# Sigmoid attention and a gated feed-forward layer on one core: score tiles in bursts of three, the last sigmoid put off, and row copies in mid-stretch

## The chip, the core and the metric

The kernel runs on one core of one Trainium2 chip. The time is device microseconds, the median of several runs. TensorE (PE) multiplies matrices, with its weight loads on a row of their own (PEld); VectorE (DVE) and ScalarE (ACT) do elementwise work and empty PSUM, the eight-bank memory that TensorE writes to; GpSimd (POOL) and SyncE (SP) here issue DMA transfers. Each engine works through its instructions in the order in which the program gives them and waits on semaphores for the others.

## What is computed

Eight batches of twelve heads, 448 positions, head size 64. Attention uses a sigmoid in place of a softmax; its output, 3584 tokens of width 768, goes through a feed-forward layer of width 2048 with a SiLU gate.

```python
scores = scale * np.matmul(q, k.transpose(0, 1, 3, 2)) - np.log(S)
attn = 1.0 / (1.0 + np.exp(-scores))
attn_out = np.matmul(attn, v)                     # (8, 12, 448, 64)
x = attn_out.transpose(0, 2, 1, 3).reshape(B * S, H * D)
h = x @ w_in                                      # (3584, 768) @ (768, 2048)
g = h * (1.0 / (1.0 + np.exp(-h)))
out = g @ w_out                                   # (3584, 2048) @ (2048, 768)
```

## The kernel before

**Attention.** Four heads at a time make a block `g`, three blocks to a batch, 24 in all; a block has seven key chunks `ch`, so there are 168 score tiles (`units`). `scores(g, ch)` (L170) issues eight matmuls of 64x64 by 448 columns, two quads of four; the four of a quad use four quarters of the TensorE array at once. A tile fills one two-bank PSUM buffer of the pool `ps_sc` (two such buffers), and one sigmoid of 128x896 on ScalarE (L184) reads it into `attnT` (12 buffers). `values(g)` (L194) multiplies the seven tiles of a block with v in 28 matmuls (L208) into two single banks, and VectorE copies them, scaled, into `xT` (L219). Matmuls of 64x64 are called scores and values here, all others dense.

**Feed-forward.** `h_unit(b, fc)` (L230) takes six dense matmuls of 448 columns (L236) into one single bank, a sigmoid on ScalarE (`tsig`, L248) and a product on VectorE (`gTr`, L249). `out_set` (L289) computes two 128-row blocks of the output in seven products instead of eight, after Strassen's scheme: VectorE forms sums `S` of blocks of `gTr` (L319, L320, L323, L328), each product is eight dense matmuls of 384 columns (L307), the first product is copied by ScalarE (`m1`, L322), and VectorE adds up the others (`plus`, L315). Sums of the weights (`T`, L278) are formed once. In two of the sets ScalarE also copies a block for later (`kept`, L375).

**PSUM.** `ps_sc` holds two buffers of two banks, `ps_1` four single banks, which take in turn the results of `h_unit`, `out_set`, `values` and of the transposes. A new tile takes the bank that, in the order of the program, was given back first.

**The order.** It is written out by hand. `all_moe` (L380) is a generator that emits the dense work of all batches one matmul (one "step") at a time and yields 189 for a step of `h_unit` and 163 for one of `out_set`. `stretch(ns)` (L399) raises `due` by ns and draws steps until `done` has reached it; `hold` keeps it drawing over the seam from the last h unit to the first product. The main loop (L534) takes two score tiles, a "burst", then at most one block of values and one row copy, and then a stretch whose length depends on the batch that the scores belong to (`paces`, L532). A long stretch of 99 steps stands ahead of the third batch (L538). Behind the last scores the rest of the dense work follows.

**The operands of the scores.** k and q are loaded by DMA from GpSimd's queue (`load`, L71; four buffers each). From block 9 on, VectorE rewrites them to rows (`dma_transpose`, L159, the copy is L163) and a DMA from SyncE's queue transposes them (L164). `after_values` (L440) puts the row copies of block g + 3 on the list `later`; `rows_if_any` (L467) takes one from it at each burst, and behind the q copy loads block g + 4.

Of the kernel before, what the change touches and what calls it, by code (L numbers as in the profile page):

```python
# [11 lines left out]
F32 = mybir.dt.float32  # L12
# [5 lines left out]
def kernel(  # L18
# [9 lines left out]
    nc = tc.nc  # L28
# [42 lines left out]
    def load(names, g, c0=0, c1=NCH):  # L71
        b, iq = divmod(g, NQ)
        for name in names:
            if (name, g) not in flat:
                new_flat(name, g)
            for half in range(2):
                h0 = half * (H // 2) + 2 * iq
                nc.gpsimd.dma_start(  # L78
                    flat[name, g][half * HP : (half + 1) * HP, :, c0:c1].rearrange(
                        "p i c d -> p i (c d)"  # L80
                    ),
                    source[name][b, h0 : h0 + 2].rearrange("i (p c) d -> p i (c d)", c=NCH)[
                        :, :, c0 * D : c1 * D
                    ],
                )
# [73 lines left out]
    def dma_transpose(g, name, copy):  # L159
        if ("k", g) not in qkT:  # L160
            new_qkT(g)
        rows = p3.tile([P, NCH, 2, D], F16, tag=f"{name}r", name=f"{name}r")
        copy(rows, flat[name, g].rearrange("p j c d -> p c j d"))  # L163
        nc.sync.dma_start_transpose(  # L164
            out=qkT[name, g], in_=rows.rearrange("p c j d -> p (c j d)")
        )

    attnT = {}

    def scores(g, ch):  # L170
        attnT[g, ch] = p12.tile([P, 2, S], F16, tag="attnT", name="attnT")
        psc = ps_sc.tile([P, 2, 512], F32, tag="pssc", name="psc")
        for half in range(2):
            own = slice(half * HP, (half + 1) * HP)
            for j in range(2):
                rows = slice(j * D, (j + 1) * D)
                nc.tensor.matmul(  # L177
                    psc[own, j, :S],
                    qkT["k", g][rows, ch, own],
                    qkT["q", g][rows, :, own],  # L180
                    start=True,
                    stop=True,
                )
        nc.scalar.activation(  # L184
            attnT[g, ch], psc[:, :, :S], AF.Sigmoid, bias=bias_s, scale=QKSCALE
        )

    xT = {}
    ready = set()
# [36 lines left out]
    pairs = [half * NQ + iq for iq in range(NQ - 1) for half in range(2)] + [NQ - 1, 2 * NQ - 1]  # L226

    hold = False

    def h_unit(b, fc):  # L230
        nonlocal hold
        hold = b > 0 and fc == NFC - 1
        ph = ps_1.tile([P, 512], F32, tag="ps1", name="ph")
        for at, cc in enumerate(pairs):
            assert b in ready or at < 4
            nc.tensor.matmul(  # L236
                ph[:, :S],
                w_in_sb[:, cc, fc * P : (fc + 1) * P],
                xT[b][:, cc, :],
                start=(at == 0),  # L240
                stop=(at == NCC - 1),
            )
            if at < NCC - 1:
                yield 189
        if fc == NFC - 1:
            h_done.add(b)
        tsig = p3.tile([P, S], F16, tag="tsig", name="tsig")
        nc.scalar.activation(tsig, ph[:, :S], AF.Sigmoid, bias=0.0, scale=ISX)  # L248
        nc.vector.tensor_mul(  # L249
            gTr[:, fc, (b % 2) * S : (b % 2) * S + S], ph[:, :S], tsig  # L250
        )
        yield 189

    rows_of = out.rearrange("(b p c) e -> b c p e", b=B, c=NCH)

# [31 lines left out]
        return [rows_of[2 * m + u // NCH, u % NCH] for u in (2 * g, 2 * g + 1)]  # L287

    def out_set(a1, rows1, a2, rows2, last=False):  # L289
        nonlocal hold  # L290
        lo, hi = slice(0, NHC), slice(NHC, NFC)
        osb = [p4.tile([P, DMODEL], F32, tag="osb", name="osb") for _ in range(2)]
        c11, c12 = (osb[0][:, nh * NO2 : (nh + 1) * NO2] for nh in range(2))
        c21, c22 = (osb[1][:, nh * NO2 : (nh + 1) * NO2] for nh in range(2))
        m1 = p2.tile([P, NO2], F32, tag="m1", name="m1")
        sg = [cpool.tile([P, NHC, P], F16, tag=f"S{i}", name=f"S{i}") for i in range(1, 5)]

        def store(rows, o, cols, engines):
            for at, (row, eng) in enumerate(zip(rows, engines)):
                eng.dma_start(row[:, cols], o[at * HP : (at + 1) * HP, cols])  # L300

        left, right, whole = slice(0, NO2), slice(NO2, DMODEL), slice(0, DMODEL)

        def product(a, w):
            po = ps_1.tile([P, 512], F32, tag="ps1", name="po")
            for fc in range(NHC):
                nc.tensor.matmul(  # L307
                    po[:, :NO2], a[:, fc, :], w[:, fc, :], start=(fc == 0), stop=(fc == NHC - 1)
                )
                if fc < NHC - 1:  # L310
                    yield 163
            return po[:, :NO2]

        def plus(o, po, x, sign=ISX):
            nc.vector.scalar_tensor_tensor(  # L315
                out=o, in0=po, scalar=sign, in1=x, op0=ALU.mult, op1=ALU.add
            )

        nc.vector.tensor_sub(sg[2], a1[:, lo], a2[:, lo])  # L319
        nc.vector.tensor_add(sg[0], a2[:, lo], a2[:, hi])  # L320
        po = yield from product(a1[:, lo], wq[0][0])
        nc.scalar.activation(m1, po, AF.Copy, scale=ISX)  # L322
        nc.vector.tensor_sub(sg[1], sg[0], a1[:, lo])  # L323
        hold = False
        yield 163
        po = yield from product(a1[:, hi], wq[1][0])
        plus(c11, po, m1)
        nc.vector.tensor_sub(sg[3], a1[:, hi], sg[1])  # L328
        if last:
            store(rows1, osb[0], left, (nc.sync, nc.sync))  # L330
        yield 163
        po = yield from product(sg[2], tw[3])
        plus(c22, po, m1)
        yield 163
        po = yield from product(sg[1], tw[2])
        plus(c22, po, c22)
        plus(c12, po, m1)
        yield 163
        po = yield from product(a2[:, hi], tw[4])
        plus(c21, po, c22, -ISX)  # L340
        yield 163
        po = yield from product(sg[0], tw[1])
        plus(c22, po, c22)
        plus(c12, po, c12)
        store(rows2, osb[1], whole, (nc.sync, nc.sync))
        yield 163
        po = yield from product(sg[3], wq[1][1])
        plus(c12, po, c12)
        if last:
            store(rows1, osb[0], right, (nc.sync, nc.scalar))  # L350
        else:
            store(rows1, osb[0], whole, (nc.sync, nc.sync))
        yield 163
# [26 lines left out]
    def all_moe():  # L380
        for m in range(B // 2):
            yield from moe_h(2 * m)
            if m > 0:
                yield from moe_set(m, 0)
            yield from moe_h(2 * m + 1)
            if m == 0:
                yield from moe_set(m, 0)
            yield from moe_set(m, 2)
            yield from moe_set(m, 4)
            if m % 2 == 1:  # L390
                g = NCH - 1
                yield from out_set(
                    kept, row_blocks(m - 1, g), block(g), row_blocks(m, g), m == B // 2 - 1
                )

    stream = all_moe()
    done = due = 0.0

    def stretch(ns):  # L399
        nonlocal done, due  # L400
        due += ns
        while done < due or hold:
            step_ns = next(stream, None)
            if step_ns is None:
                break
            done += step_ns

    first_k = load_first_k()
    new_flat("k", 0)
# [30 lines left out]
    def after_values(g):  # L440
# [20 lines left out]
            load("kq", 9)  # L461
        if g >= 6 and g + 3 < NQB:
            later.extend(((g + 3, "k"), (g + 3, "q")))

    later = []

    def rows_if_any():  # L467
        if later:
            g, name = later.pop(0)
            dma_transpose(g, name, nc.vector.tensor_copy)  # L470
            if name == "q" and g + 4 < NQB and g + 4 > 12:
                load("kq", g + 4)

    def values_if_any():
        if waiting:
# [53 lines left out]
        for do, *what in behind.get(n, ()):  # L529
            do(*what)  # L530

    paces = {1: 1600, 2: 2000, 3: 2550, 4: 3400, 5: 3400, 6: 3000, 7: 3000}  # L532
    stretch(paces[1])
    for n in range(NT_B + 3, len(units), 2):  # L534
        burst = units[n : n + 2]
        if n == 2 * NT_B:
            values_if_any()
            stretch(21500)  # L538
        for u in burst:
            scores(*u)  # L540
        values_if_any()
        rows_if_any()
        for g, ch in burst:
            if ch == NCH - 1:
                waiting.append(g)
        if n in (24, 30):
            transposes(4 + (n - 24) // 6, "k")
        elif n in (26, 32):
            transposes(4 + (n - 26) // 6, "q")
        stretch(paces[1] if 1 not in ready else paces[n // NT_B])  # L550
    for g in waiting:
        values(g)
    for _ in stream:
# [31 lines left out]
```

## Time and profile before

| | |
|---|---|
| median of 3 runs | 382.56 us (382.36 to 382.85) |
| the profiled execution | 382.75 us, of which the span of the instructions is 381.0 |
| h steps, L236 | 768 matmuls of 128x448 |
| output steps, L307 | 784 matmuls of 128x384 |
| score and value matmuls, L177 and L208 | 672 and 672, 64x64 by 448 |
| score sigmoid, L184 | 168 of 128x896, mean 1016 ns, 158.9 us |
| tsig, L248, and its product, L249 | 128 each, mean 545 and 623 ns |
| sums of products, L315 | 112, mean 555 and 552 ns |
| xT, L219 | 48, mean 619 ns |
| row copies, L163 | 30 on VectorE, mean 610 ns |
| k loads, q loads | median 5.5 and 5.8 us from issue to landing |

The kernel has an opening of some 77 us, in which the weights are loaded, the first batches' scores run almost alone and the long stretch of 99 h steps ends. From there to about 325 us bursts and dense stretches take turns. The rest, to 377 us, is dense work alone. A row of the profile shows start, duration, engine, line, operation and count; consecutive instructions of one kind are merged. Durations of matmuls overlap since they are pipelined, so the time that a matmul takes up is read from one start to the next.

### The profile page before, as it was taken

Reading aid. Unit: us, or ns where it says so; the run is one execution under the profiler, and the core shown is the slowest. Engines: PE = TensorE matmul, PEld = TensorE weight load, DVE = VectorE, ACT = ScalarE, POOL = GpSimd, SP = SyncE. Lnnn points to the kernel's source line nnn. Section 1 sums busy time; section 2 is a strip of 40 time slices with the busy share of each in tenths; the row PEclk is TensorE's granted clock in tenths of the full one; section 3 lists DMA queues with packets and bytes.
Section 4 is the critical chain, followed back from the end, with each engine's and each line's share of the span. In section 5 each row is a group of like instructions: output and inputs, shape, how many; then the busy total and the mean of one; then the engine's idle time right before and its main releaser. Section 6 shows DMA issues by size and latency. Waiting matters only on the chain.

```text
span 381.0 us, 7663 instructions
## 1 busy us (share of the span) xinstructions
PE 372.2 (98%) x3083; PEld 186.9 (49%) x3083; DVE 233.8 (61%) x415; ACT 240.0 (63%) x328; POOL 92.9 (24%) x158
## 2 busy tenths in 40 slices
PE   7999999999999999999999999999999999999995
PEld 2444445545554445444555444544455444555663
DVE  2446646996565666556767547735857446656773
ACT  4998886758777875778444686577774787044000
POOL 8855326202752323121311303101100000000000
PEclk9999999999999999999999999999999999999999
DMA  7999999974999936937939859535346300110233
GB/s 112 180 188 204 205 203 181 155 103 101 166 236 232 141 51 97 184 47 75 152 68 191 96 112 122 56 101 74 48 77 105 83 3 2 41 41 2 75 92 83
DMA packets 66403, 42.71 MB, mean 112 GB/s; under 512 B 37056, under 2 KB 62912, under 8 KB 66368
## 3 DMA queue, kind: packets, MB, share of 16 engines
q0 software_dynamic: 28032, 22.69, 42.7%
q1 hardware_dynamic: 38112, 19.31, 28.2%
q8 instruction: 24, 0.39, 0.4%
q10 hardware_dynamic: 224, 0.23, 0.2%
q14 instruction: 11, 0.09, 0.1%
HBM read 45.61 MB, written 11.01 MB: 149 GB/s over the span
## 4 chain that ended last, share of the span: by engine, by line
PE 80%; DMA 12%; DVE 2%; ACT 2%; POOL 1%; issue 1%; DVEq 0%
PE po L307 34%; PE ph L236 29%; PE psc L177 9%; PE pav L208 6%; DMA w_in_sb<-in_moe_w_in_dram 6%; DMA w_out_sb<-in_moe_w_out_dram 5%; DVE gTr L249 1%; DMA ks<-in_k_dram 1%; ACT attnT L184 1%; DMA vf<-in_v_dram 1%; DVE T L278 1%; POOL qf L78 1%; PE pw L135 1%; POOL kf L78 0%; ACT qr L138 0%
## 5 line engine op out<-in xcount | busy, mean ns | idle before, releaser
L184 ACT ACTIVATE attnT<-psc,bias_s 128x896 f16<-128x896 f32 x168 | 158.9, 1016 | 53.3 <-PE psc L177 53.2
L236 PE MATMUL ph<-xT,w_in_sb 128*128 128x448 f16 x768 | 153.2, 353 | 0.0
L249 DVE TENSOR_TENSOR gTr<-ph,tsig 128x448 f16<-128x448 f32 x128 | 78.1, 623 | 72.0 <-ACT tsig L248 71.4
L236 PEld LDWEIGHTS <-w_in_sb 128*128 128x128 f16 x768 | 71.9, 98 | 75.7 <-issue 12.9
L248 ACT ACTIVATE tsig<-ph 128x448 f16<-128x448 f32 x128 | 68.2, 545 | 47.8 <-PE ph L236 46.2
L78 POOL DMA_DIRECT2D vf<-in_v_dram x48 | 28.7, 613 | 140.7 <-PE pav L208 140.2
L307 PEld LDWEIGHTS <-S 128*128 128x128 f16 x448 | 42.3, 98 | 33.9 <-issue 6.8
L315 DVE SCALAR_TENSOR_TENSOR osb<-po,osb 128x384 f32<-128x384 f32 x70 | 37.7, 555 | 25.1 <-PE po L307 24.5
L177 PE MATMUL psc<-qT,kT 64*64 64x448 f16 x672 | 50.4, 362 | 2.5 <-ACT attnT L184 1.2
L219 DVE TENSOR_SCALAR xT<-pav 128x448 f16<-128x448 f32 x48 | 27.7, 619 | 30.3 <-PE pav L208 30.3
L307 PE MATMUL po<-T,S 128*128 128x384 f16 x224 | 40.6, 327 | 0.1
L307 PEld LDWEIGHTS <-gTr 128*128 128x128 f16 x304 | 28.7, 98 | 23.4 <-issue 5.2
L307 PE MATMUL po<-w_out_sb,S 128*128 128x384 f16 x224 | 39.9, 326 | 0.0
L208 PE MATMUL pav<-attnT,vf 64*64 64x448 f16 x672 | 37.9, 349 | 0.4 <-DVE gTr L249 0.4
L78 POOL DMA_DIRECT2D qf<-in_q_dram x48 | 28.9, 612 | 38.1 <-DVE qr L163 16.9
L307 PE MATMUL po<-w_out_sb,gTr 128*128 128x384 f16 x192 | 34.7, 327 | 0.0
L177 PEld LDWEIGHTS <-kT 64*64 64x64 f16 x672 | 15.0, 104 | 32.8 <-issue 30.9
L78 POOL DMA_DIRECT2D kf<-in_k_dram x48 | 28.9, 612 | 7.0 <-DVE kr L163 4.4
L208 PEld LDWEIGHTS <-vf 64*64 64x64 f16 x672 | 20.2, 107 | 12.4 <-issue 1.9
L315 DVE SCALAR_TENSOR_TENSOR osb<-po,m 128x384 f32<-128x384 f32 x42 | 23.2, 552 | 4.1 <-PE po L307 2.5
L322 ACT ACTIVATE m<-po 128x384 f32<-128x384 f32 x14 | 6.9, 491 | 23.7 <-PE po L307 23.7
L307 PE MATMUL po<-T,gTr 128*128 128x384 f16 x112 | 21.4, 326 | 0.0
(40 smaller groups left out, 131.0 us busy)
## 6 DMA issues: line engine op xcount, KB each, us to landing
out_dram<-osb SPq DMA_DIRECT2D x54, 192.0 KB, 2.9
qf<-in_q_dram POOLq DMA_DIRECT2D x48, 112.0 KB, 5.8
vf<-in_v_dram POOLq DMA_DIRECT2D x48, 112.0 KB, 4.8
kf<-in_k_dram POOLq DMA_DIRECT2D x46, 112.0 KB, 5.5
w_in_sb<-in_moe_w_in_dram POOLq DMA_DIRECT2D x4, 768.0 KB, 10.5
w_out_sb<-in_moe_w_out_dram POOLq DMA_DIRECT2D x4, 768.0 KB, 17.0
kT<-kr SPq DMA_TRANSPOSE x18, 5.6
qT<-qr SPq DMA_TRANSPOSE x18, 6.2
```

The costliest lines, as they stand in the source:

```text
L78: nc.gpsimd.dma_start(flat[name, g][half * HP : (half + 1) * HP, :, c0:c1].rearrange("p i c d -> p i (c d)"), source[name][b, h0 : h0 + 2] ...
L135: nc.tensor.matmul(pw, dummy[:, :P], dummy, start=True, stop=True)
L177: nc.tensor.matmul(psc[own, j, :S], qkT["k", g][rows, ch, own], qkT["q", g][rows, :, own], start=True, stop=True,)
L184: nc.scalar.activation(attnT[g, ch], psc[:, :, :S], AF.Sigmoid, bias=bias_s, scale=QKSCALE)
L208: nc.tensor.matmul(pav[half][j * D : (j + 1) * D, :S], flat["v", g][own, j, ch, :], at[own, j, :], start=(ch == 0), stop=(ch == NCH - 1),)
L219: nc.vector.tensor_scalar_mul(xT[b][:, half * NQ + iq, :], pav[half][:, :S], SX)
L236: nc.tensor.matmul(ph[:, :S], w_in_sb[:, cc, fc * P : (fc + 1) * P], xT[b][:, cc, :], start=(at == 0), stop=(at == NCC - 1),)
L248: nc.scalar.activation(tsig, ph[:, :S], AF.Sigmoid, bias=0.0, scale=ISX)
L249: nc.vector.tensor_mul(gTr[:, fc, (b % 2) * S : (b % 2) * S + S], ph[:, :S], tsig)
L307: nc.tensor.matmul(po[:, :NO2], a[:, fc, :], w[:, fc, :], start=(fc == 0), stop=(fc == NHC - 1))
L315: nc.vector.scalar_tensor_tensor(out=o, in0=po, scalar=sign, in1=x, op0=ALU.mult, op1=ALU.add)
L322: nc.scalar.activation(m1, po, AF.Copy, scale=ISX)
```

## The change

A burst has three score tiles in the batches that `TILES` names, and two in the second and fourth batch and wherever a block of values is due in the burst. In a burst of three the first tile goes into two single banks of `ps_1`, read by two sigmoids of 128x448; the other two use `ps_sc`. The sigmoid of the third is put off: it is issued behind the next tsig or m1, or when the stretch has drawn more than 1300 ns of steps, or at the stretch's end. In `stretch` an h step now counts 0.72 of its 189 ns (from the third batch on) and an output step 1.28 of its 163, so there are fewer steps between bursts among output steps and more among h steps. `hold` sets in one h unit earlier from the third batch on. The long stretch keeps its length. Besides the row copy at the burst, another is taken from `later` in the middle of each stretch. The output's arithmetic is the same.

```diff
-    def scores(g, ch):
+    late = []
+
+    def late_sigmoid():
+        while late:
+            to, psc = late.pop()
+            nc.scalar.activation(to, psc, AF.Sigmoid, bias=bias_s, scale=QKSCALE)
+
+    def scores(g, ch, banks=None, put_off=False):
         attnT[g, ch] = p12.tile([P, 2, S], F16, tag="attnT", name="attnT")
-        psc = ps_sc.tile([P, 2, 512], F32, tag="pssc", name="psc")
+        if banks is None:
+            psc = ps_sc.tile([P, 2, 512], F32, tag="pssc", name="psc")
+            banks = [psc[:, j] for j in range(2)]
+            parts = [(attnT[g, ch], psc[:, :, :S])]
+        else:
+            parts = [(attnT[g, ch][:, j], banks[j][:, :S]) for j in range(2)]
...
-        nc.scalar.activation(
-            attnT[g, ch], psc[:, :, :S], AF.Sigmoid, bias=bias_s, scale=QKSCALE
-        )
+        if put_off:
+            late.extend(parts)
+            return
+        for to, psc in parts:
+            nc.scalar.activation(to, psc, AF.Sigmoid, bias=bias_s, scale=QKSCALE)
+
+    def single_banks():
+        return [ps_1.tile([P, 512], F32, tag="ps1", name="psc1") for _ in range(2)]
...
     def h_unit(b, fc):
-        nonlocal hold
-        hold = b > 0 and fc == NFC - 1
+        nonlocal hold, weight
+        weight = H_WEIGHT if b > 1 else 1.0
+        hold = b > 1 and fc >= NFC - 2 or b == 1 and fc == NFC - 1
...
         nc.scalar.activation(tsig, ph[:, :S], AF.Sigmoid, bias=0.0, scale=ISX)
+        late_sigmoid()
...
+    H_WEIGHT, SET_WEIGHT = 0.72, 1.28
...
     def out_set(a1, rows1, a2, rows2, last=False):
-        nonlocal hold
+        nonlocal hold, weight
+        weight = SET_WEIGHT
...
         nc.scalar.activation(m1, po, AF.Copy, scale=ISX)
+        late_sigmoid()
...
     def stretch(ns):
         nonlocal done, due
         due += ns
+        middle = due - ns / 2
+        since = 0
         while done < due or hold:
             step_ns = next(stream, None)
             if step_ns is None:
                 break
-            done += step_ns
+            done += step_ns * weight
+            since += step_ns
+            if since > 1300:
+                late_sigmoid()
+            if done > middle:
+                rows_if_any()
+                middle = math.inf
+        late_sigmoid()
...
-    paces = {1: 1600, 2: 2000, 3: 2550, 4: 3400, 5: 3400, 6: 3000, 7: 3000}
-    stretch(paces[1])
-    for n in range(NT_B + 3, len(units), 2):
-        burst = units[n : n + 2]
-        if n == 2 * NT_B:
-            values_if_any()
-            stretch(21500)
-        for u in burst:
-            scores(*u)
+    TILES = {2: 3, 3: 2, 4: 3, 5: 3, 6: 3, 7: 3}
+    paces = {1: 1600, 2: 2400, 3: 2550, 4: 3500, 5: 3300, 6: 3100, 7: 2900}
+    def burst(n, tiles):
+        new = units[n : n + (tiles if not waiting else 2)]
+        for i, u in enumerate(new):
+            single = i == len(new) - 3
+            scores(*u, single_banks() if single else None, len(new) == 3 and i == 2)
         values_if_any()
         rows_if_any()
-        for g, ch in burst:
-            if ch == NCH - 1:
-                waiting.append(g)
+        waiting.extend(g for g, ch in new if ch == NCH - 1)
+        return len(new)
...
+    values_if_any()
+    stretch(21500)
+    n = 2 * NT_B
+    while n < len(units):
+        ns = paces[n // NT_B]
+        tiles = burst(n, TILES[n // NT_B])
+        n += tiles
+        stretch(ns * tiles / 2)
```

More of the change, by code (lines that the diff above doesn't have):

```diff
@@ L177, in scores @@
                 nc.tensor.matmul(
-                    psc[own, j, :S],
+                    banks[j][own, :S],
                     qkT["k", g][rows, ch, own],
@@ L228 @@
     hold = False
+    weight = 1.0
     def h_unit(b, fc):
-        nonlocal hold
-        hold = b > 0 and fc == NFC - 1
+        nonlocal hold, weight
+        weight = H_WEIGHT if b > 1 else 1.0
+        hold = b > 1 and fc >= NFC - 2 or b == 1 and fc == NFC - 1
         ph = ps_1.tile([P, 512], F32, tag="ps1", name="ph")
@@ L394, in all_moe, with rows_if_any @@
                 )
+    later = []
+    def rows_if_any():
+        if later:
+            g, name = later.pop(0)
+            dma_transpose(g, name, nc.vector.tensor_copy)
+            if name == "q" and g + 4 < NQB and g + 4 > 12:
+                load("kq", g + 4)
     stream = all_moe()
@@ L463, in after_values @@
             later.extend(((g + 3, "k"), (g + 3, "q")))
[L465 to L472, printed above, removed]
     def values_if_any():
@@ L530 @@
             do(*what)
-    paces = {1: 1600, 2: 2000, 3: 2550, 4: 3400, 5: 3400, 6: 3000, 7: 3000}
-    stretch(paces[1])
-    for n in range(NT_B + 3, len(units), 2):
-        burst = units[n : n + 2]
-        if n == 2 * NT_B:
-            values_if_any()
-            stretch(21500)
-        for u in burst:
-            scores(*u)
+    TILES = {2: 3, 3: 2, 4: 3, 5: 3, 6: 3, 7: 3}
[5 more added lines that the diff above has]
+            scores(*u, single_banks() if single else None, len(new) == 3 and i == 2)
         values_if_any()
         rows_if_any()
-        for g, ch in burst:
-            if ch == NCH - 1:
-                waiting.append(g)
+        waiting.extend(g for g, ch in new if ch == NCH - 1)
+        return len(new)
+    stretch(paces[1])
+    for n in range(NT_B + 3, 2 * NT_B, 2):
+        burst(n, 2)
         if n in (24, 30):
@@ L549 @@
             transposes(4 + (n - 26) // 6, "q")
-        stretch(paces[1] if 1 not in ready else paces[n // NT_B])
+        stretch(paces[1])
+    values_if_any()
[6 more added lines that the diff above has]
+        stretch(ns * tiles / 2)
     for g in waiting:
```

## The prediction

> **What bounds the kernel now.** First the page's busy shares, then who TensorE waited for, then its timeline in the dense part, then ScalarE and VectorE beside it.
>
> ```profile
> span 381.0 us, 7663 instructions
> PE 372.2 (98%) x3083; PEld 186.9 (49%) x3083; DVE 233.8 (61%) x415; ACT 240.0 (63%) x328; POOL 92.9 (24%) x158
> ...
> PEclk9999999999999999999999999999999999999999
> ```
> ```profile
> PE psc L177 <- ACT attnT L184: 1.2, 4, 0.5
> ...
> PE pav L208 <- DVE gTr L249: 0.4, 1, 0.4
> ```
> TensorE is busy for 98% at a full granted clock, and its waits for other engines sum to a few us, most of them in the first 80. Pipelined busy time says nothing of lost steps, so I read starts:
>
> ```profile
> 204.87 0.57 PE L177 MATMUL psc<-qT,kT 64*64 64x448 f16 x8
> 205.37 1.96 PE L307 MATMUL po<-T,S 128*128 128x384 f16 x11
> ...
> 208.89 0.57 PE L177 MATMUL psc<-qT,kT 64*64 64x448 f16 x8
> 209.29 1.49 PE L208 MATMUL pav<-attnT,vf 64*64 64x448 f16 x28
> 210.72 2.45 PE L307 MATMUL po<-w_out_sb,S 128*128 128x384 f16 x14
> ...
> 214.74 3.58 PE L236 MATMUL ph<-xT,w_in_sb 128*128 128x448 f16 x18
> 218.25 0.57 PE L177 MATMUL psc<-qT,kT 64*64 64x448 f16 x8
> ```
> ```profile
> 331.14 18.32 PE L236 MATMUL ph<-xT,w_in_sb 128*128 128x448 f16 x96
> 349.30 2.76 PE L307 MATMUL po<-w_out_sb,gTr 128*128 128x384 f16 x16
> 351.90 2.76 PE L307 MATMUL po<-T,S 128*128 128x384 f16 x16
> ```
> Undisturbed, an h step takes (349.30 - 331.14)/96 = 0.189 us and an output step 2.60/16 = 0.163. The 18 h steps from 214.74 take 3.51 to the next score matmul, 18 x 0.189 = 3.41 and 0.10 over; the start records give 0.283 from an h step to a score step, so 0.094 over, and 0.256 from an output step, 0.093 over. That is the way into the 64x64 shape. A burst of two tiles lasts 0.503 to the next dense step (204.87 to 205.37), of which the first quad of four concurrent matmuls takes 0.212 by the records and the last, with the way out, 0.291. With the 28 value matmuls it is 1.83 (208.89 to 210.72). Apart from these switches every dense step after 80 us is at its floor, with two exceptions, one of which is this:
>
> ```profile
> 143.78 0.38 PE L177 MATMUL psc<-qT,kT 64*64 64x448 f16 x4
> 144.64 0.38 PE L177 MATMUL psc<-qT,kT 64*64 64x448 f16 x4 [0.48 <-ACT attnT L184]
> 144.95 0.50 PE L307 MATMUL po<-w_out_sb,gTr 128*128 128x384 f16 x2
> ```
> Two bursts stand six output steps apart, the second score buffer is still being read, and the burst lasts 1.17 for 0.50: 0.67 lost. The other is 0.23 at 79.7, where the third product waits for its VectorE difference (L319). So TensorE is the limit, and only switches and these 0.90 can be won.
>
> **The switches saved.** Everything up to the first 99 h steps stays in the same order (77 us of the span), and so does what follows the last scores. In between, TensorE's instruction order of the built kernels, counted, has 63 bursts of two before and 50 after, 26 of three and 24 of two. Groups of 64x64 work: before 46 score bursts x 0.503 + 17 with values x 1.827 + one of values alone 1.42 = 55.6 us, and 64 ways in x 0.094 = 6.0. After: 26 x (0.503 + 0.212) = 18.6, 6 x 0.503 = 3.0, 16 x 1.827 = 29.2, one score-value-score group 1.827 + 0.424 = 2.25, 1.42, sum 54.5; 50 ways in, 4.7. Difference **2.42 us**. The third quad has no row of its own; the bounds are 0.188 (a value quad, (1.42 - 0.10)/7) and 0.291 (a last quad), and I take 0.212, the same pair of operations one quad earlier.
>
> **The other edits by themselves.** 26 tiles are read by two 128x448 sigmoids in place of one 128x896: at best 2 x 0.44 (start to start after a tsig, 214.34 to 214.78) against 0.895 between four in a row (below), at worst 2 x 0.545 against 1.016, 0.07 more each, at most 1.9 us of ScalarE's 140 idle ones. The weights, paces and `hold` issue nothing; they move bursts. The 30 row copies on VectorE (0.61), their 30 DMA transposes on SP and the loads they release on POOL are the same in number; the second of each pair moves to the middle of a stretch, past VectorE's next product sums, SP's output stores and POOL's loads. With 61% of VectorE busy this is free unless a bank waits behind it, which is priced next.
>
> **New waits on the path.** ScalarE's and VectorE's timelines give durations in a queue:
>
> ```profile
> 142.69 3.70 ACT L184 ACTIVATE attnT<-psc,bias_s 128x896 f16<-128x896 f32 x4
> ```
> ```profile
> 210.82 1.16 DVE L219 TENSOR_SCALAR xT<-pav 128x448 f16<-128x448 f32 x2 [1.59 <-PE pav L208]
> 211.90 0.61 DVE L163 COPY kr<-kf 128x896 f16<-128x896 f16 x1
> 212.42 1.67 DVE L315 SCALAR_TENSOR_TENSOR osb<-po,osb 128x384 f32<-128x384 f32 x3
> ```
> Four sigmoids in 3.70: 0.895 from one to the next, 1.016 for the last. xT 0.54 each, a row copy 0.52, then a product sum of 0.555. A sigmoid starts 0.49 after its burst's first matmul (208.89 to 209.39). A long burst's late sigmoid therefore ends at 0.49 + 2 x 0.45 + 0.895 + 1.016 = 3.30 after the burst began. The tightest spacing is 17 output steps: the next burst begins at 0.715 + 17 x 0.163 + 0.094 = 3.58, its second quad at 3.79, its third at 4.00. That is clear, with these exceptions, found by laying each burst's waits against those sums:
> - Twice a `kept` copy (L375, 0.56 in a queue) stands before the late sigmoid and the next burst is a short one: ready at 3.86 + 0.04, wanted at 3.79: 0.11 x 2 = 0.22. Queued behind it are only that burst's values, which are late by the same.
> - In the one score-value-score group, m1 of the product that just ended goes first (ends 0.50 after), two sigmoids end at 0.50 + 0.895 + 1.016 = 2.41 + 0.04, and the second tile wants its buffer at 0.42 + 1.32 + 0.21 = 1.95: 0.50.
> - Once a long burst follows values after 12 output steps (12 x 0.163 + 0.094 = 2.05), and its second single bank is freed by a sum that stands behind two xT and the k copy: 0.10 + 2 x 0.54 + 0.52 + 0.555 + 0.04 = 2.30: 0.25. The q copy now comes behind this sum, not before it.
> - At h steps a single bank is freed 1.40 after its h unit ended (tsig 0.20 later, 0.545, product 0.62, in the records); the closest burst comes 1.47 after: 0 to 0.05, taken as 0.05.
> These sum to 1.02. Gone are the 0.67 at 143.78, since those bursts move apart, and the 0.23 at 79.7, since the first burst now comes after 14 output steps and the difference is finished within it.
>
> **Sum**, against the profiled execution's 382.75: 382.75 - 2.42 + 1.02 - 0.90 = 380.45. The median of the runs, 382.56, is 0.19 lower than that execution: 380.26, so **380.3 us**. If none of the new waits arose it would be 379.2; with all at the rival's prices 381.9.
>
> **The rivals.**
> *ScalarE sets the pace of the long bursts.* Three tiles need three times 0.9 there while TensorE needs 0.715. With the mean durations of the page (1.016, 0.545, 0.634, 0.555) in place of queued ones: the two `kept` places lose 0.50 each, the score-value-score group 0.71, a pair of long bursts 14 steps apart 0.24, the single-bank places 0.49 and 0.23, in sum 2.67 and a gain of 0.65: 381.9. For it: in the 17-step stretches ScalarE would be busy 2.8 to 3.4 of 3.58. Against: four in a row took 3.70, not 4.06. The Trainium skill (TensorEngine Tiling (Array Packing), PSUM Bottleneck) speaks for it: packing small matmuls speeds TensorE and not the emptying of PSUM, which may become the limit. By that rule the time is this 381.9; the trace bears it out at 143.78 alone.
> *The general banks run short.* Two of four are lent to a tile, and 12 of the 26 long bursts take one whose source ended under 2.2 us before. If evacuation took there what the slowest tenth takes now by the records (2.0 for an h unit, 1.75 for a product), 1.3 would go: 381.6.
> *The change does not save the switch.* If the third quad costs 0.291 like a last one, 26 x 0.08 = 2.1 goes: 382.4, no change.
> *Slower: a row copy that waits for its load blocks VectorE.* Loads are otherwise four blocks ahead, but those of block 10 are issued on POOL right behind the values of block 6, and its k copy is now due 8.8 us after those (10.4 before, 102.58 against 92.2), ahead of the sum that frees the single bank of the 12-step place. The second half of k was issued at 94.39 and landed after 6.24, which is 8.4 after the values; the copy is due 0.4 later. Each us later is a us on TensorE: from a landing of about 8.9 us on, the kernel is slower than before. k loads issued from 104 to 112 took up to 8.6, a q transpose 10.5; at 10.5 it is 3.9 more: 384.2. Against it: the loads ahead of it on POOL do not change.
>
> **How the numbers follow.** Forecast 0.62, own range 379.6 to 381.2; ScalarE 0.13; banks 0.08; no switch saved 0.07; slower 0.08; 0.02 for better still. Within 0.2% (0.8 us, about what a measurement of this kernel can tell) lie the third rival and half of the first, 0.07 + 0.065, and of the forecast's share I count 0.06 there and 0.02 as slower, for a wait that the sums above overlook: same 0.20, slower 0.10, faster 0.70. The range reaches from no new waits, 379.2, to just past the third rival, 382.5.
>
> **What would show it.** Right: 50 bursts after the first 99 h steps, long ones of 0.71 us with 0.094 before them, h and output steps at 0.189 and 0.163, and waits of score matmuls for ScalarE of about 0.7 in all behind 77 us. Wrong: long bursts above 0.8 as a rule, h or output steps that wait at their first matmul, a row copy that VectorE waits 1 us or more for near 101, or a late sigmoid that ends after the next burst's third quad.

## The result, and the profile after

The changed kernel takes 379.84 us, the median of six runs (379.45 to 380.55); the kernel before, on the same chip, takes 382.46 (six runs, 382.21 to 382.85). The ratio is 0.9932, with a 95% interval of 0.9919 to 0.9945: faster by 2.6 us. The profiled execution took 379.95 us. The page of the changed kernel, its span, busy shares and granted clock:

```profile
span 378.2 us, 7694 instructions
...
PE 369.5 (98%) x3083; PEld 189.9 (50%) x3083; DVE 234.0 (62%) x415; ACT 243.0 (64%) x354; POOL 93.3 (25%) x158
...
PEclk9999999999999999999999999999999999999999
```

The span is shorter by 2.8 us, the clock is as full as before, and TensorE still has its 3083 matmul instructions and 98%. ScalarE has 26 instructions more, one for each tile that two sigmoids read. Whom TensorE waited for, in us, times and longest:

```profile
PE psc L191 <- ACT attnT L202: 1.1, 4, 0.4
...
PE pav L227 <- DVE gTr L271: 0.4, 1, 0.4
```

By this list next to nothing has changed, so the gain is not in waits that went. It is in what the list does not count, and that is read from starts, in the timeline of TensorE (start, duration, engine, line, operation, tiles, shape, count):

```profile
198.04 0.76 PE L191 MATMUL psc<-qT,kT 64*64 64x448 f16 x12
198.74 1.31 PE L333 MATMUL po<-w_out_sb,S 128*128 128x384 f16 x7
...
202.74 0.76 PE L191 MATMUL psc<-qT,kT 64*64 64x448 f16 x12
203.43 2.61 PE L333 MATMUL po<-T,S 128*128 128x384 f16 x15
...
207.28 0.57 PE L191 MATMUL psc<-qT,kT 64*64 64x448 f16 x8
207.68 1.49 PE L227 MATMUL pav<-attnT,vf 64*64 64x448 f16 x28
209.10 2.77 PE L333 MATMUL po<-w_out_sb,S 128*128 128x384 f16 x16
```

A score tile is one quad: `scores` issues four matmuls (672 for 168 tiles), not the eight in two quads that "The kernel before" gives. A block of values is seven quads. A burst of three lasts from 198.04 to 198.74 and from 202.74 to 203.43: 0.694 by the unrounded records, the median and the least of 26. The burst of two still lasts 0.505. So the third tile costs 0.694 - 0.505 = 0.189, and what remains of a burst when its quads are taken off is 0.505 - 2 x 0.189 = 0.127. Two score tiles with the 28 value matmuls fit the same line: nine quads are 9 x 0.189 + 0.127 = 1.83, and 207.28 to 209.10 is 1.82. The way in is 0.098, read over a whole dense stretch as what it takes to the next score matmul beyond 0.189 and 0.163 a step: 0.094 of it at the last step, the rest mostly at the first, which takes 0.01 longer. Together, a stay in the 64x64 shape costs **0.225 us, however long it is, and 0.189 for each quad**. The price goes with the shape and not with a change of operands: inside a stay the step from scores to values takes 0.189, and the last h step before an output step takes 0.189 too. There were 64 stays, now there are 50.

What else changed are the waits that a group of 64x64 work or a dense stretch shows beyond these floors. From the end of the first 99 h steps to the last scores they sum to 1.11 us before and 1.45 after. Four of them are larger than 0.1 us. The one group in which scores, values and scores follow each other, on TensorE:

```profile
139.78 0.57 PE L191 MATMUL psc<-qT,kT 64*64 64x448 f16 x8
140.18 1.49 PE L227 MATMUL pav<-attnT,vf 64*64 64x448 f16 x28
141.51 0.36 PE L191 MATMUL psc<-qT,kT 64*64 64x448 f16 x4
142.22 0.38 PE L191 MATMUL psc<-qT,kT 64*64 64x448 f16 x4 [0.36 <-ACT attnT L202]
142.54 0.66 PE L333 MATMUL po<-w_out_sb,gTr 128*128 128x384 f16 x3
```

From 139.78 to 142.54 are 2.76 us for 11 quads, which need 2.21: 0.55 lost. The bracket names ScalarE, which is reading the buffer that the last tile wants. The second place, on ScalarE:

```profile
271.56 0.65 ACT L402 ACTIVATE kept<-gTr 128x512 f16<-128x512 f16 x1
272.08 1.02 ACT L175 ACTIVATE attnT<-psc,bias_s 128x896 f16<-128x896 f32 x1
```

The late sigmoid (L175) stands behind a `kept` copy and ends at 273.10, while the next burst began at 272.71: that burst with its values takes 2.09 for 1.83. At 97.41 the same costs 0.20. The fourth, on VectorE and then on TensorE:

```profile
99.54 1.16 DVE L238 TENSOR_SCALAR xT<-pav 128x448 f16<-128x448 f32 x2 [1.98 <-PE pav L227]
100.61 0.61 DVE L163 COPY kr<-kf 128x896 f16<-128x896 f16 x1
101.14 0.55 DVE L341 SCALAR_TENSOR_TENSOR osb<-po,osb 128x384 f32<-128x384 f32 x1
```
```profile
101.50 1.00 PE L191 MATMUL psc<-qT,kT 64*64 64x448 f16 x12
102.43 1.15 PE L333 MATMUL po<-w_out_sb,S 128*128 128x384 f16 x6
```

The sum that frees the lent bank ends at 101.69, and the burst that wants it began at 101.50: 0.93 for 0.694, 0.24 lost.

### The profile page after: what moved, and what is told of

It reads as the page before. It is cut to its first block, busy times and chain, and to the rows that moved or that the text cites. A ratio compares the mean times of both kernels' runs of the same rounds, so it can differ in the third digit from the quotient of the medians.

```text
span 378.2 us, 7694 instructions
## 1 busy us (share of the span) xinstructions
PE 369.5 (98%) x3083; PEld 189.9 (50%) x3083; DVE 234.0 (62%) x415; ACT 243.0 (64%) x354; POOL 93.3 (25%) x158
## 4 chain that ended last, share of the span: by engine, by line
PE 90%; ACT 6%; DMA 1%; issue 1%; DVE 1%; DVEq 0%; ACTq 0%
PE ph L257 39%; PE po L333 34%; PE psc L191 9%; PE pav L227 7%; ACT attnT L202 6%; DMA ks<-in_k_dram 1%; PE ptrk L148 0%; PE ptrq L148 0%; ACT m L348 0%; ACT attnT L175 0%; DVE qT L155 0%; DVE gTr L271 0%; DVE osb L341 0%; PE pw L135 0%; DVE kf L469 0%
## 5 line engine op out<-in xcount | busy, mean ns | idle before, releaser
L202 ACT ACTIVATE attnT<-psc,bias_s 128x896 f16<-128x896 f32 (+1 forms) x168 | 138.0, 902 | 41.3 <-PE psc L191 41.2
L257 PE MATMUL ph<-xT,w_in_sb 128*128 128x448 f16 x768 | 150.9, 353 | 0.0
L257 PEld LDWEIGHTS <-w_in_sb 128*128 128x128 f16 x768 | 72.9, 98 | 73.5 <-issue 8.3
L191 PE MATMUL psc<-qT,kT 64*64 64x448 f16 x672 | 48.6, 360 | 2.4 <-ACT attnT L202 1.1
L78 POOL DMA_DIRECT2D qf<-in_q_dram x48 | 29.1, 621 | 27.4 <-DMA w_out_sb<-in_moe_w_out_dram 12.4
L191 PEld LDWEIGHTS <-kT 64*64 64x64 f16 x672 | 16.8, 105 | 30.5 <-issue 26.8
L175 ACT ACTIVATE attnT<-psc,bias_s 128x896 f16<-128x896 f32 x26 | 26.6, 1022 | 0.0
```

What stands on the lines that cost most here:

```text
L78: nc.gpsimd.dma_start(flat[name, g][half * HP : (half + 1) * HP, :, c0:c1].rearrange("p i c d -> p i (c d)"), source[name][b, h0 : h0 + 2] ...
L175: nc.scalar.activation(to, psc, AF.Sigmoid, bias=bias_s, scale=QKSCALE)
L191: nc.tensor.matmul(banks[j][own, :S], qkT["k", g][rows, ch, own], qkT["q", g][rows, :, own], start=True, stop=True,)
L202: nc.scalar.activation(to, psc, AF.Sigmoid, bias=bias_s, scale=QKSCALE)
L257: nc.tensor.matmul(ph[:, :S], w_in_sb[:, cc, fc * P : (fc + 1) * P], xT[b][:, cc, :], start=(at == 0), stop=(at == NCC - 1),)
```

## The experiments

Each is the changed kernel with the edit shown. "Groups" are the stays of TensorE in the 64x64 shape behind the first 99 h steps, "waits" what they and the dense stretches between them take beyond 0.189 a quad or h step, 0.163 an output step and 0.225 a group, all read from starts. A table of all of them stands at the end.

### e1_no_mid_rows: no row copy in the middle of a stretch

```diff
-            if done > middle:
-                rows_if_any()
-                middle = math.inf
```


> The changed kernel without the second row copy in mid-stretch; TensorE's order is the same. Theory (the gain is switches saved, less waits): 379.8, within 0.3 of the changed kernel, since 50 bursts still consume the 30 copies two blocks ahead of use, and long bursts stay at 0.69. Rival (earlier transposes are part of the gain): scores wait for transposes, at least 0.8 slower, 380.6 or more.

Measured: 379.86 us (379.66 to 380.23), ratio 0.9928 (0.9914 to 0.9941). The same time as the changed kernel: these copies are no part of the gain, and a cost of theirs does not show either. The one difference in its waits is the long burst after the 12 output steps, which loses 0.54 for 0.24, since the k copy on VectorE starts 0.26 later. That copy, and the time from issue to landing of the two halves of its load:

```profile
100.87 0.62 DVE L163 COPY kr<-kf 128x896 f16<-128x896 f16 x1 [0.20 <-issue]
```
```profile
DMA to landing us min/median/max: 4.6/5.7/6.9
```

The second half was issued at 93.92 and landed 6.87 us later, at 100.80, just ahead of the copy at 100.87. In the changed kernel it landed at 100.02, 0.59 ahead of its copy. The view names no releaser, but these times fit a copy that waits for its load: the way of the prediction's fourth rival, at a price of 0.3 us.

### e2_no_put_off: the third sigmoid at once

```diff
-            scores(*u, single_banks() if single else None, len(new) == 3 and i == 2)
+            scores(*u, single_banks() if single else None)
```


> The changed kernel with the third tile's sigmoid issued at once. Theory: the two places where a kept copy stands ahead of the late sigmoid lose nothing any more (0.20 and 0.26 in the trace), and the tsig that now stands behind it still ends about 0.9 before its bank is wanted: 379.4. Rival (putting off protects the h units' banks): h steps wait behind long bursts, 7 to 9 of those by about 0.3, 382 or so; at least 0.8 slower.

Measured: 379.41 us (378.96 to 380.05), ratio 0.9917 (0.9903 to 0.993). The intervals overlap with the change's, so the times alone do not tell them apart. The trace does. ScalarE at the first of the two places:

```profile
94.45 2.95 ACT L202 ACTIVATE attnT<-psc,bias_s 128x448 f16<-128x448 f32 x4 [0.76 <-PE psc L191]
97.28 0.64 ACT L402 ACTIVATE kept<-gTr 128x512 f16<-128x512 f16 x1
```

The `kept` copy now stands behind all sigmoids of the burst, and the groups at both places take 1.83: the 0.20 and the 0.26 are gone. In this order of bursts, putting the sigmoid off costs some 0.4 us, and no wait of that size came in its place (the burst at 101.47 loses 0.07 more).

### e3_pairs_spaced: everything but the bursts of three

```diff
-    TILES = {2: 3, 3: 2, 4: 3, 5: 3, 6: 3, 7: 3}
+    TILES = {b: 2 for b in range(2, 8)}
```


> The changed kernel with two tiles in every burst, everything else (weights, paces, hold, row copies, late sigmoid) kept: 63 bursts, 73 ways into the 64x64 shape in place of 61. Theory: 13 bursts more x 0.19 = 2.5 more, and where hold is overdrawn bursts follow each other after 0, 1 and 3 output steps and wait for ScalarE, by sums 0.5, 0.5, 1.5, 1.15 and 0.7, less about 1.0 of the changed kernel's own waits: 384 to 386, with the waits of scores for ScalarE in the trace at 4 or more. Rival (the spacing by stage, which relieves ScalarE, is what wins): no slower than 381.

Measured: 385.56 us (385.31 to 385.98), ratio 1.0077 (1.0065 to 1.009): slower than before. TensorE was in the 64x64 shape 62 times, 12 more than with threes, worth 12 x 0.225 = 2.70, and its waits are 4.6 us, 3.15 more; 5.85 in sum, and the medians differ by 5.72. The list of waits, of whose 4.3 us 3.3 in seven waits lie behind 77 us, and the worst place in the timeline:

```profile
PE psc L191 <- ACT attnT L202: 4.3, 11, 0.7
```
```profile
236.30 0.57 PE L191 MATMUL psc<-qT,kT 64*64 64x448 f16 x8
236.81 0.34 PE L333 MATMUL po<-w_out_sb,gTr 128*128 128x384 f16 x1
237.85 0.38 PE L191 MATMUL psc<-qT,kT 64*64 64x448 f16 x4 [0.70 <-ACT attnT L202]
238.75 0.38 PE L191 MATMUL psc<-qT,kT 64*64 64x448 f16 x4 [0.51 <-ACT attnT L202]
```

After a single output step the next pair follows, and both of its tiles wait for the sigmoids of the last. So there is no gain without the bursts of three: the rest of the change by itself loses 3 us.

### e4_threes_plain: the bursts of three without the spacing

```diff
-        hold = b > 1 and fc >= NFC - 2 or b == 1 and fc == NFC - 1
+        hold = b > 0 and fc == NFC - 1
-    H_WEIGHT, SET_WEIGHT = 0.72, 1.28
+    H_WEIGHT, SET_WEIGHT = 1.0, 1.0
-    paces = {1: 1600, 2: 2400, 3: 2550, 4: 3500, 5: 3300, 6: 3100, 7: 2900}
+    paces = {1: 1600, 2: 2000, 3: 2550, 4: 3400, 5: 3400, 6: 3000, 7: 3000}
```


> Bursts of three with the late sigmoid and the mid-stretch copies, but steps counted at their plain 189 and 163, hold and paces as in the kernel before: 50 bursts, 62 ways in. Theory: nearly the whole gain, 379.5 to 380.5 (one way in more, 0.19; 0.67 lost again where two bursts stand six output steps apart; the 0.5 of the score-value-score group and the kept waits gone). Rival (spacing by stage carries the gain, since among h steps ScalarE has no room for three tiles): waits of h units, 381.5 or more.

Measured: 382.87 us (382.61 to 383.91, 11 runs), ratio 1.0008 (0.9999 to 1.0017): no gain at all. My theory fell here. It had 51 groups, as expected, and 4.4 us of waits. The rival's size came true, but its reason, that among h steps ScalarE has no room for three tiles, holds for some 1.5 of the 4.4 us only. First a place where it does not hold, the long burst at 259.75, first on VectorE, then on ScalarE, then on TensorE:

```profile
258.85 0.61 DVE L163 COPY qr<-qf 128x896 f16<-128x896 f16 x1
259.38 0.61 DVE L271 TENSOR_TENSOR gTr<-ph,tsig 128x448 f16<-128x448 f32 x1
```
```profile
259.66 0.54 ACT L269 ACTIVATE tsig<-ph 128x448 f16<-128x448 f32 x1 [0.59 <-PE ph L257]
260.46 1.16 ACT L202 ACTIVATE attnT<-psc,bias_s 128x448 f16<-128x448 f32 x2 [0.25 <-PE psc L191]
```
```profile
259.75 1.05 PE L191 MATMUL psc<-qT,kT 64*64 64x448 f16 x12
260.73 0.36 PE L257 MATMUL ph<-xT,w_in_sb 128*128 128x448 f16 x1
```

ScalarE is idle before both of its operations, so here it has room. The burst lasts 0.98 for 0.694 since its lent bank still holds an h unit, and the product that reads it (gTr) stands behind a row copy on VectorE until 259.99. Six long bursts lose 1.99 us to a late reader of a lent bank, at 102.80, 187.19, 259.75, 265.38, 285.89 and 307.14. At 265.38 and 307.14 (0.14 and 0.21) it is late on account of ScalarE: the late sigmoid starts there at 262.82 and 304.65, and the tsig follow it without a gap. The pair at 143.78 loses the 0.67 that it lost before the change, other groups 0.25. Where a new set of output steps begins, its third product waits twice for a VectorE difference, whose `gTr` is late because the late sigmoid stands between two tsig on ScalarE: 0.55 each. The 0.22 near 79 is back too.

### e5_plain_count_new_hold: as e4, with the change's hold

```diff
-        hold = b > 0 and fc == NFC - 1
+        hold = b > 1 and fc >= NFC - 2 or b == 1 and fc == NFC - 1
```
The diff is against e4. 

> As e4 (steps counted plain, paces of before), but with hold set one h unit earlier as in the change; 51 bursts' groups. In e4 twelve waits took 4.2, of which 1.1 at two seams from h units to products with a burst nine h steps ahead. Theory (switches saved, less waits that depend on where each burst stands): the seams' 1.1 goes, the rest stays, 381.3 to 382.2. Rival (the earlier hold is what the spacing owes its effect to): 380.2 or less.

Measured: 382.31 us (381.74 to 383.74, 12 runs), ratio 0.9996 (0.9983 to 1.0008). The two waits of 0.55 are gone, others of 0.4 and 0.1 came, and 3.8 us of waits are left. So about 0.6 of the 3 us between e4 and the changed kernel go with `hold`, and the rest, 2.5, with the weights and paces, which were not tried apart. The intervals of e4 and e5 overlap; it is the waits, 4.40 and 3.78, that tell them apart.

### e6_ones: one tile in each burst

```diff
-    TILES = {2: 3, 3: 2, 4: 3, 5: 3, 6: 3, 7: 3}
+    TILES = {b: 1 for b in range(2, 8)}
```


> One tile to a burst where the change has two or three, paces halved with the tiles; 105 groups of 64x64 work behind the opening, against 64 before and 50 in the changed kernel. Theory: a group costs its two switches whatever it holds: 82 x 0.291 + 5 x 0.503 + 17 x 1.83 + 1.42 and 105 x 0.094, 68.7 against 61.7 before, 7 more, and about 2 of waits where bursts follow each other at the seams: 389.5 to 391.5, with single-tile bursts at 0.29. Rival (a switch costs nothing of its own, the shorter queue on ScalarE pays): 384 or less.

Measured: 393.87 us (393.58 to 394.13), ratio 1.029 (1.027 to 1.031), 2.4 us above the range. The timeline:

```profile
155.78 0.38 PE L191 MATMUL psc<-qT,kT 64*64 64x448 f16 x4
156.10 1.31 PE L333 MATMUL po<-w_out_sb,S 128*128 128x384 f16 x7
```

A burst of one lasts 0.316, where I had expected the 0.29 of a last quad: 0.189 + 0.127, on the line of the others. Over 82 such bursts 0.025 more is 2.1 us. With 105 groups, 55 x 0.225 = 12.4 us come to the changed kernel's time, and 1.55 of waits (3.0 for 1.45): 379.84 + 13.9 = 393.8. So the price read from the starts of the changed kernel also gives the time of a kernel with 55 stays more.

### e7_waits_removed and e8_threes_everywhere: the waits taken away

Not put off; a burst that also has values takes no row copy; after the long stretch each stretch has at least 11 steps. e8 has at least 14 steps and bursts of three in all batches.

```diff
-        while done < due or hold:
+        steps = 0
+        while done < due or hold or steps < min_steps:
+            steps += 1
...
-            scores(*u, single_banks() if single else None, len(new) == 3 and i == 2)
+            scores(*u, single_banks() if single else None)
+        if not waiting:
+            rows_if_any()
         values_if_any()
-        rows_if_any()
...
+    min_steps = 11
```


> The changed kernel with its four largest waits taken away: the third sigmoid not put off (kept places, 0.20 and 0.26), the burst's row copy left to mid-stretch where values are due (single bank behind the k copy, 0.22), and a stretch of at least 11 steps (the score-value-score group, 0.51, for one more way in, 0.19). Theory: 379.84 - 1.0 = 378.8, no wait of a score matmul above 0.1 behind 77 us. Rival (the waits hide others that come up in their place): 379.4 or more.

> As e7, with a least stretch of 14 steps and bursts of three in the fourth batch too: 49 groups, 30 of them of three. Theory: 0.45 less than e7 in switches (58.30 against 58.75), 378.4 to 379.2, as h bursts of that batch load ScalarE to 94%. Rival (ScalarE has no room there): h steps wait, 379.8 or more.

Measured: e7 378.69 us (378.42 to 378.95), ratio 0.9893 (0.9876 to 0.991); e8 378.63 (378.39 to 379.05), ratio 0.989 (0.9874 to 0.9907). Both beat the kernel before and, by about 1.2 us, the changed one. The list of waits of e7, and its timeline where the changed kernel had its one group of scores, values and scores:

```profile
PE psc L191 <- ACT attnT L202: 0.8, 3, 0.4
```
```profile
138.83 0.57 PE L191 MATMUL psc<-qT,kT 64*64 64x448 f16 x8
139.23 1.49 PE L227 MATMUL pav<-attnT,vf 64*64 64x448 f16 x28
140.66 1.47 PE L333 MATMUL po<-w_out_sb,gTr 128*128 128x384 f16 x8
```

The three waits of the list all lie in the opening. The values are followed by output steps now, and from 77 us to the last scores no wait over 0.05 is left. That costs one group more (51), 0.225. e8 has 49 groups, 0.45 less, but 0.4 more waits (0.23 at 319.44, 0.11 twice at h steps): nothing is won.

### e9_plain_no_mid and e10_plain_fixed: is it the spacing, or only its waits?

e9 is e4 without the copies in the middle (the diff is against e4); e10 is e4 with the change's hold, without those copies, without the putting off, and with the least number of steps of e7, here `min_steps = 13`.

```diff
-            if done > middle:
-                rows_if_any()
-                middle = math.inf
```


> As e4_threes_plain (bursts of three, groups weighted alike and the old hold), but with no row copy in the middle of a stretch. My theory: of e4's 4.2 us of waits, those of the long bursts at 187.19, 259.75, 265.38 and 307.14 (0.24 + 0.29 + 0.14 + 0.21 = 0.9) stood behind a row copy on VectorE and go; the two seams (0.55 each), the 0.67 at 143.78 and the 0.71 at 102.80 may stay. So about 382.0 us (381.5 to 382.5). Rival, that the long bursts wait because ScalarE has no room when they stand this close: unchanged, 382.6 us or more, with the long bursts still waiting for 0.2 us and more each.

> Bursts of three with groups weighted alike (the old spacing), but with the waits seen in e4 taken away one by one: the new hold, no row copy in the middle of a stretch, the third sigmoid not put off, and the lent bank not asked for within 13 output steps of a long stretch. My theory: the spacing by stage is worth something only through the waits that it keeps off, so this runs in 379.0 to 379.8 us, as the changed kernel does, with no more than 0.7 us of waits behind 77 us. Rival, that spacing by stage itself carries the gain (ScalarE or the tiles' readiness needs it): 381.5 us or more, with score tiles that wait for a sigmoid in many bursts.

Measured: e9 382.47 us (382.05 to 386.57, 11 runs), ratio 1.0011 (0.9992 to 1.0031), and e10 381.74 (381.09 to 383.56, 12 runs), ratio 0.9985 (0.9974 to 0.9996). In e9 the waits at 187 and 259.75 are gone, as expected; those at 265 and 307 are not (0.14 at 264.73 and 0.21 at 306.50), so these need no row copy: their `gTr` is late behind the sigmoids on ScalarE, as in e4. e10 missed: 3.06 us of waits, not 0.7. The rival's time, 381.5 or more, came true. Its sign, score tiles that wait for a sigmoid in many bursts, shows in one burst (0.40 at 237.74). Most of the rest are lent banks again (0.65 at 102.92, 0.40 at 284.54, 0.23 at 263.93) and h steps. On ScalarE and TensorE of e10:

```profile
302.26 1.91 ACT L202 ACTIVATE attnT<-psc,bias_s 128x896 f16<-128x896 f32 x2
304.04 1.86 ACT L269 ACTIVATE tsig<-ph 128x448 f16<-128x448 f32 x4
```
```profile
302.29 2.62 PE L257 MATMUL ph<-xT,w_in_sb 128*128 128x448 f16 x13
305.31 1.10 PE L257 MATMUL ph<-xT,w_in_sb 128*128 128x448 f16 x5 [0.40 <-DVE gTr L271]
```

Among the h steps, three tiles' sigmoids keep the tsig behind them until 304.04, the h banks run out, and TensorE loses 0.57 there and 0.22 near 310. At the same two bursts, with the same 16, 24 and 24 h steps around them, e5 puts the third sigmoid off, and on its ScalarE one tsig goes first:

```profile
305.18 0.56 ACT L269 ACTIVATE tsig<-ph 128x448 f16<-128x448 f32 x1
305.61 1.03 ACT L175 ACTIVATE attnT<-psc,bias_s 128x896 f16<-128x896 f32 x1
306.50 1.44 ACT L269 ACTIVATE tsig<-ph 128x448 f16<-128x448 f32 x3
```

There no h step waits, and the lent bank at 308.10 costs 0.21. So putting the sigmoid off saves some 0.6 us at these two bursts, where in the changed kernel (e2) it only costs. The parts do not add up one by one: plain spacing keeps 3 us or more of waits with each of these sets of edits. e7, with a set that is similar but not the same (it keeps the copies in the middle, and takes none in bursts with values), leaves 0.20 on the spacing by stage. Whether some plain spacing without waits exists was not tried.

### All runs by groups and waits

The last column but one is e7's 378.69 + 0.225 x (groups - 51) + (waits - 0.20).

| kernel | groups | waits, us | worked out, us | measured, us |
|---|---|---|---|---|
| before | 64 | 1.11 | 382.53 | 382.46 |
| changed | 50 | 1.45 | 379.72 | 379.84 |
| e1 no copies in the middle | 50 | 1.74 | 380.01 | 379.86 |
| e2 not put off | 50 | 1.06 | 379.33 | 379.41 |
| e3 pairs, spaced by stage | 62 | 4.60 | 385.57 | 385.56 |
| e4 threes, plain spacing | 51 | 4.40 | 382.89 | 382.87 |
| e5 the same, new hold | 51 | 3.78 | 382.27 | 382.31 |
| e6 ones | 105 | 3.00 | 393.64 | 393.87 |
| e7 waits removed | 51 | 0.20 | 378.69 | 378.69 |
| e8 threes everywhere | 49 | 0.62 | 378.66 | 378.63 |
| e9 e4, no copies in the middle | 51 | 3.93 | 382.42 | 382.47 |
| e10 plain, four edits | 51 | 3.06 | 381.55 | 381.74 |

Groups and waits from one profile of each kernel give all twelve medians within 0.25 us, over a range of 15 us. The opening is not in this sum: the profiled execution of e5 took 383.42 us, 1.1 above its median, and its first 99 h steps begin at 59.05, those of e4 at 57.95.

## Why the prediction was right

- **The switches saved** were the mechanism, and this term was too small. The 14 groups less are worth 14 x 0.225 = 3.15 us, where the prediction has 2.42. The step that was off is the third quad at 0.212, "the same pair of operations one quad earlier": it costs 0.189, next to the lower of its two bounds (0.188, a value quad). The records show where 0.212 belongs: 0.213 is the time from the first quad of a stay to its second, once in each stay, and every quad between the first and the last takes 0.189. In the kernel before, the nine quads of scores and values showed that already. The long burst is 0.694 for 0.715, and 26 x 0.021 is 0.55 of the 0.73; the way in (0.098 over a stretch, for 0.094), the short burst (0.505 for 0.503) and the mixed group make the rest.
- **The new waits** came at the places named but for one, and were 1.25, not 1.02: the two `kept` places 0.20 and 0.26 (0.11 each predicted), the mixed group 0.55 (0.50), the lent bank after 12 output steps 0.24 (0.25), none at h steps (0.05).
- **The old waits**, 0.67 and 0.23, are gone as predicted. The sum with the measured terms is 382.75 - 3.15 + 1.25 - 0.90 = 379.95, the profiled execution's own time. The two sizes that were off, 0.73 and 0.23, partly cancelled, which is luck; the forecast was 0.5 us high.
- **"The weights, paces and hold issue nothing; they move bursts"** is true and was read too lightly. The prediction gives the gain to the switches and the 0.90 of old waits, and but for these it does not say what the spacing keeps off. By e4 the switches saved by themselves are eaten whole by waits when the steps are counted as before. The prediction's sum holds because the waits were laid against the actual order of the built kernel.
- **The copies in the middle** show no cost, by e1. **The second sigmoid of a split tile** was undervalued: ScalarE is busy 171.66 us from 77 to 325 us, 168.65 before, 3.0 more for 26 sigmoids, against at most 1.9 in the prediction. It is off the path but for the places above.
- **ScalarE as the pace**: only the named places show it, 0.20 + 0.26 + 0.55 = 1.01 us (about 0.7 was predicted), and no pair of long bursts 17 steps apart waits 0.05 or more. The Trainium skill (TensorEngine Tiling (Array Packing), PSUM Bottleneck) says that packing speeds TensorE and not the emptying of PSUM. In the change the trace agrees at these places alone; in e3 it agrees at more, with 3.3 us in seven waits for ScalarE behind 77 us.
- **General banks** did not run short for dense steps in the changed kernel: no dense stretch took over 0.03 us more than its floor, and the one lent bank that came late is the 0.24 above; in e10 they did (0.57 and 0.22). **The switch not saved** is excluded by 0.694. **The load that comes late** did not show in the changed kernel: the k copy started at 100.61, right behind xT, and its load had landed 0.59 before. By e1 it is near: there a landing 0.78 us later cost 0.3.

## What to carry to other kernels

Count how often TensorE changes its shape and price a change by starts, not by busy time: here a stay costs 0.225 us whatever is in it, so fewer and longer stays pay, and one line through the two group sizes of the kernel before would have given the third. Then lay each longer burst against whoever last reads the bank that it borrows, operation by operation in that engine's queue, since bursts of three gave 2.6 us or nothing by where they stood. When waits are removed one at a time, read the new trace for those that come in their place before adding up.

## What the runs showed of the hardware

- In the middle of a stay, four concurrent 64x64 matmuls of 448 columns take the time of one 128x128 matmul of 448 columns, 0.189 us; stays of one, two, three and nine quads take 0.316, 0.505, 0.694 and 1.829. Their ends carry the price: 0.213 from the first quad to the second and 0.291 from the last to the next dense step. The Trainium skill (TensorEngine Tiling (Array Packing), Key Properties) says that changing the tiling mode drains TensorE. The trace agrees in that each stay costs 0.225 us for both ways together; the draining itself no run here shows.
- The granted clock was 1.00 from 77 to 325 us in the kernel before and in the changed one, so their difference is not one of clock.
